# One product moved between two units of a Strassen stage, and new orders for its units

## The chip, the cores and the metric

The kernel runs on one core of a Trainium2 chip, as one launch. The metric is the device time of that launch in microseconds (us); the median of three runs is given. Matrix work is done by TensorE (PE), everything else by VectorE (DVE), ScalarE (ACT) and GpSimd (POOL); SyncE (SP) issues most of the transfers.

## The reference

A short causal convolution over time feeds a two-layer network with a hard-swish between. All arrays are float32.

```python
# x: (8, 4096, 192), weight: (8 heads, 7 taps)
w = softmax(weight, axis=-1)                  # exp(w - max), / (sum + 1e-9)
out[b, s, h, g] = sum_k w[h, k] * x_pad[b, s + k, h, g]   # 6 zeros ahead in time
x = out.reshape(32768, 192)

h = x @ w_in                                  # w_in (192, 2048)
g = h * clip(h + 3, 0, 6) / 6
return g @ w_out                              # w_out (2048, 192)
```

## The kernel before, in words

**Blocks.** The 32768 tokens are cut into 32 blocks of 1024. Block 0 is computed plainly, while the weights are still being prepared; blocks 1 to 31 all go through the same two stages, one after the other: the *h stage* (`h_phase`, lines 404 to 418), which makes `g`, and the *output stage* (`out_strassen`, lines 586 to 624; `out_last` for the last block), which makes the result and, on VectorE, the convolution of the next block.

**Two streams.** The 192 channels lie as three thirds of 64 rows. Rows 0 to 63 of the arrays hold the lower 512 tokens of a block and the lower half of `w_in`'s 2048 columns; rows 64 to 127 hold the upper ones. A matmul of the h stage (`half_mm`, line 303) uses 64 rows, so two run side by side on TensorE: stream **L** on the lower 64 rows, stream **U** on the upper 64. Each stream needs both token halves; a copy of `y` with the halves swapped (`OTHER`) is made by two transfers per block.

**Units and operations.** A *unit* is 2 x 128 columns of `w_in` for each stream; there are four (`UNITS`), numbered 1 to 4 here (0 to 3 in the code). The class `Unit` (line 355) has one object for each unit and stream. In a unit, the first two thirds of the channels are multiplied by Strassen's scheme with seven products instead of eight (`P1` to `P7`), on sums prepared of `y` (`YS1` to `YS4`) and of the weights (`w_in_t`). The last third is added plainly by `K11`, `K12`, `K21`, `K22`. That makes 11 products in a stream and unit, 44 in a stream and stage, each [64 x 128] by [64 x 512], into one of the eight PSUM banks. The operations have short names, with the stream's letter before them:

- `P1`: starts the bank of result a. `F1` (ScalarE, line 385): copies P1 from bank to bank, as the start of result b. `P6` accumulates onto that copy, so it waits for `F1`.
- `P5`: a bank of its own. `CE` (ScalarE, line 388): copies P5 to memory (`p5`, three buffers) and gives its bank back.
- `AF` and `AD` (VectorE, line 392): add P5 to what stands in b's bank, and write the sum as the start of result f, or d. `P7` goes onto b between the two, so it waits for `AF`; `K22` goes onto d and waits for `AD`. `P4` and `K21` finish b.
- `Ra`, `Rf`, `Rb`, `Rd` (ScalarE, line 317): the clipped factor of a result. `Ga`, `Gf`, `Gb`, `Gd` (VectorE, line 321): the gate, which multiplies by it, writes `g`, and gives the bank back.

Banks are handed out in the order in which they were given back (`take`, `give`, lines 297 to 301): which operation gives a bank that another takes follows from the order of the plan.

**What sets the order.** The order is written out by hand. `PLAN` (line 349) is a list of steps such as `LP6`; `h_phase` goes through it once for each unit and calls `run`, so each engine's instructions stand in its queue in this order. A step with `'` belongs to the unit before, so the last products and gates of a unit lie in the next unit's pass; such steps do nothing in the first pass, and a fifth pass at the end runs them alone. `X` runs what is left of the block before: its last transpose and its stores.

For the first unit of a stage, then, TensorE's queue begins `LP1 UP1 LP5 UP5 LP6 UP6 LP2 UK11`, and ScalarE's `LF1 UF1 LCE UCE`. From the second unit on, `LP4'` and `UP4'` of the unit before lie between P1 and P6 as well.

**The output stage** uses all 128 rows and a quarter of the columns for each of four products side by side (`mm`, line 423, recorded at line 427). It has 168 matmuls, needs both streams' results, and follows the h stage in TensorE's queue.

Of the kernel before, what the change touches and what calls it, by code (L numbers as in the profile page):

```python
# [16 lines left out]
def kernel(  # L17
# [101 lines left out]
    UNITS = NP // 2  # L119
# [214 lines left out]
    def h_out(c, group, bs, between):  # L334
# [11 lines left out]

    PLAN = """
        LP1 LRd' UP1 LGd' LP4' UP4' URd' LF1 LP5 UGd' UF1 UP5 LP6 UP6 LP2 LCE UCE LRb'  # L350
        UK11 LAF UAF LK11 X URb' UP2 LP7 LGb' UP7 LK12 UP3 UGb' LAD LP3 LRa URa LRf UK12
        UAD UGa LGa LK22 UK22 URf LGf UGf LK21 UK21
    """.split()

    class Unit:

# [45 lines left out]
                give(b)  # L402

    def h_phase(left):
        last = None
        for u in range(UNITS + 1):
            now = [Unit(u, k) for k in range(2)] if u < UNITS else None
            for step in PLAN:
                if step == "X":
                    while left:  # L410
                        left.pop(0)()
                    continue
                which = last if step[-1] == "'" else now
                if which:
                    which["LU".index(step[0])].run(step[1:].rstrip("'"))
            if last:
                g_sums(nc.gpsimd, (1, 3), range(2 * u - 2, 2 * u), 2)
            last = now

    def dff_half(k):  # L420
        return g[:, :, k // G, k % G]
# [55 lines left out]
    def g_sums(engine, which, slots, width):  # L477

        forms = {
            1: (S1, A21, A22, ALU.add), 3: (S3, A11, A21, ALU.subtract),  # L480
            2: (S2, S1, A11, ALU.subtract), 4: (S4, A12, S2, ALU.subtract),
        }
        for n in which:
            o, a, b, op = forms[n]
            for p in slots[::width]:
                r = slice(p, p + width)
                engine.tensor_tensor(out=o[:, r], in0=a[:, r], in1=b[:, r], op=op)  # L487
# [155 lines left out]
    with tc.manual_schedule():  # L643
# [106 lines left out]
        for i in range(1, NB):  # L750
            h_phase(left)
            if i + 1 < NB:
                left = out_strassen(i, conv_units(i + 1, [slice(0, K3)]))
            else:
                out_last(i)
            if i + 2 < NB:
                x_tiles[i + 2] = load_x(i + 2)
# [33 lines left out]
```

## Time and profile before

| | |
|---|---|
| time, median of 3 runs | 2425.71 us (2425.64 to 2425.78) |
| span of the profiled execution | 2423.9 us |
| TensorE's granted clock | 1.00 |
| h stage of a block, line 311 | 38.57 us |
| output stage of a block, line 427 | 36.19 us |
| VectorE busy in one h stage | 31.41 us |
| ScalarE busy in one h stage | 27.82 us |
| VectorE busy in one output stage | 33.72 us |

A page of the profile names groups of instructions by the line that issues them: L311 are all the h stage's matmuls, L427 those of the output stage, L385 the copies F1, L388 the copies CE, L392 AF and AD, L317 the clipped factors, L321 the gates. PE are the matmuls and PEld the weight loads that precede them. Each float32 matmul is recorded as two passes with a weight load each, and a few per cent of the records are missing. [...]the distance between starts says how fast they follow each other. "PE busy" is the time in which at least one matmul runs: two streams side by side and one stream alone look the same there.

### The profile page before, as it was taken

What the parts mean: (1) busy time and instruction counts of PE and PEld (TensorE: products, weight loads), DVE (VectorE), ACT (ScalarE), POOL (GpSimd) and SP (SyncE); (2) the same over time, 40 slices, a digit from 0 to 9 for tenths busy, and PEclk for the clock granted to TensorE, in tenths of its full rate; (3) what the DMA queues carried; (4) which work ended last, traced back from release to release, by engine and by line L of the source; (5) the groups of instructions that cost most, each with busy time, mean ns of one, the idle gap of its engine ahead of it and who ended that gap; (6) DMA issues with size and microseconds to landing.
All of it is one profiled execution on the core that took longest, in us unless ns stands there. A gap on an engine that the chain in (4) does not pass through costs nothing.

```text
span 2423.9 us, 40261 instructions
## 1 busy us (share of the span) xinstructions
PE 2413.0 (100%) x16468; PEld 1042.4 (43%) x16468; DVE 2088.9 (86%) x2534; ACT 1066.5 (44%) x1827; POOL 669.4 (28%) x280
## 2 busy tenths in 40 slices
PE   9999999999999999999999999999999999999998
PEld 4334444444444444443444444444444444344443
DVE  8788888988888888898888898888898888888886
ACT  7234553345443355433454334543345443355433
POOL 2423321233221333122332223322233312333122
PEclk9999999999999999999999999999999999999999
DMA  5211122201122111221112211122201122111210
GB/s 144 40 28 26 27 40 40 40 18 28 35 40 40 21 33 27 40 40 22 32 27 40 40 34 21 25 40 40 40 17 35 29 40 40 21 33 27 40 27 14
DMA packets 227338, 84.67 MB, mean 35 GB/s; under 512 B 205456, under 2 KB 210576, under 8 KB 227152
## 3 DMA queue, kind: packets, MB, share of 16 engines
q1 hardware_dynamic: 225848, 81.56, 17.1%
q8 instruction: 129, 2.11, 0.4%
q14 instruction: 57, 0.47, 0.1%
q10 hardware_dynamic: 1208, 0.27, 0.1%
q0 software_dynamic: 96, 0.26, 0.0%
HBM read 31.72 MB, written 25.17 MB: 23 GB/s over the span
## 4 chain that ended last, share of the span: by engine, by line
PE 99%; DVE 1%; DMA 0%; issue 0%; ACTq 0%; SPq 0%; DVEq 0%
PE psum L311 51%; PE psum L427 48%; DVE y L263 0%; DMA x<-in_x_dram 0%; DMA y<-y 0%; DVE c L531 0%; ACTq L92 0%; DVE scale L174 0%; DVE y L259 0%; DVE scale L195 0%; DVE sig L199 0%; DVE top L178 0%; DVE xt L537 0%; SPq L276 0%; DVEq L259 0%
## 5 line engine op out<-in xcount | busy, mean ns | idle before, releaser
L427 PE MATMUL psum<-g,w_out 128*32 128x512 f32 x9312 | 1163.6, 592 | 0.0
L311 PE MATMUL psum<-y,w_in 64*128 64x512 f32 x3664 | 957.2, 591 | 3.1 <-DVE y L263 1.7
L487 POOL TENSOR_TENSOR s<-g 128x1024 f32<-128x1024 f32 x124 | 293.4, 2366 | 1659.4 <-DVE g L321 1615.9
L317 ACT ACTIVATE r<-psum,half 128x512 f32<-128x512 f32 x1024 | 634.6, 688 | 241.6 <-PE psum L311 238.8
L427 PEld LDWEIGHTS psum<-g,w_out 128*32 128x32 f32 x9312 | 337.4, 110 | 811.7 <-issue 762.7
L321 DVE SCALAR_TENSOR_TENSOR g<-r,psum 128x512 f32<-128x512 f32 x1024 | 643.1, 681 | 4.4 <-ACT r L317 1.1
L427 PE MATMUL psum<-s,w_out 128*32 128x512 f32 x1488 | 638.5, 592 | 0.0
L311 PEld LDWEIGHTS psum<-y,w_in 64*128 64x128 f32 x3664 | 476.8, 187 | 345.0 <-issue 327.9
L311 PE MATMUL psum<-y,w_in_t 64*128 64x512 f32 x1984 | 610.2, 592 | 0.0
L392 DVE TENSOR_TENSOR psum<-psum,p 128x512 f32<-128x512 f32 x496 | 321.5, 694 | 198.7 <-PE psum L311 194.0
L263 DVE SCALAR_TENSOR_TENSOR y<-x,c_sb,y 128x1536 f32<-128x1536 f32 (+1 forms) x210 | 416.8, 1992 | 6.6
L523 ACT COPY c<-psum 32x512 f32<-32x512 f32 x188 | 108.9, 579 | 600.5 <-PE psum L427 511.7
L311 PEld LDWEIGHTS psum<-y,w_in_t 64*128 64x128 f32 x1984 | 280.1, 187 | 209.2 <-issue 142.4
L487 POOL TENSOR_TENSOR g<-g 128x1024 f32<-128x1024 f32 x124 | 336.2, 2711 | 9.7
L531 DVE TENSOR_TENSOR c<-c,psum 32x512 f32<-32x512 f32 (+1 forms) x187 | 128.1, 685 | 95.7 <-ACT c L523 89.8
L427 PEld LDWEIGHTS psum<-s,w_out 128*32 128x32 f32 x1488 | 162.4, 110 | 1.2 <-issue 1.2
L388 ACT COPY p<-psum 128x512 f32<-128x512 f32 x248 | 135.0, 587 | 61.8 <-PE psum L311 61.1
L385 ACT COPY psum<-psum 128x512 f32<-128x512 f32 x248 | 131.4, 571 | 62.3 <-PE psum L311 56.7
L487 DVE TENSOR_TENSOR g<-s,g 128x2048 f32<-128x2048 f32 x62 | 141.2, 2319 | 2.1 <-PE psum L427 2.1
L487 DVE TENSOR_TENSOR g<-g 128x2048 f32<-128x2048 f32 x62 | 139.4, 2289 | 2.3 <-PE psum L427 1.3
L591 ACT COPY c<-psum 96x512 f32<-96x512 f32 x30 | 17.5, 582 | 188.5 <-PE psum L427 188.5
L596 ACT COPY c<-psum 96x512 f32<-96x512 f32 x30 | 17.5, 583 | 170.0 <-PE psum L427 170.0
(46 smaller groups left out, 432.4 us busy)
## 6 DMA issues: line engine op xcount, KB each, us to landing
out_dram<-xt SPq DMA_DIRECT2D x382, 64.0 KB, 2.0
y<-y SPq DMA_DIRECT2D x62, 384.0 KB, 4.9
x<-in_x_dram SPq DMA_DIRECT2D x55, 388.5 KB, 5.9
stage<-in_moe_w_in_dram SPq DMA_DIRECT2D x16, 192.0 KB, 4.5
stage<-in_moe_w_out_dram SPq DMA_DIRECT2D x8, 384.0 KB, 5.6
x<-in_x_dram SPq DMA_DIRECT2D x7, 384.0 KB
y<-y SPq DMA_DIRECT2D x6, 128.0 KB, 2.4
x<-in_x_dram SPq DMA_DIRECT2D x2, 128.0 KB, 4.4
```

Of the source, the lines that this page charges most:

```text
L263: nc.vector.scalar_tensor_tensor(out=to, in0=x[:, part, k + t : k + t + W], scalar=c, in1=to, op0=ALU.mult, op1=ALU.add,)
L311: nc.tensor.matmul(out=psum[:, b], lhsT=w[r], rhs=y[r, third_of_y], start=start, stop=stop, skip_group_check=onto,)
L317: nc.scalar.activation(r6, h, ACT.Relu, bias=half[:], scale=1.0 / 6.0)
L321: nc.vector.scalar_tensor_tensor(out=out, in0=r6, scalar=1.0, in1=h, op0=ALU.min, op1=ALU.mult)
L385: nc.scalar.copy(out=psum[:, bank["b"]], in_=psum[:, bank["a"]])
L388: nc.scalar.copy(out=self.p5[:], in_=psum[:, bank["e"]])
L392: nc.vector.tensor_tensor(out=psum[:, to], in0=psum[:, bank["b"]], in1=self.p5[:], op=ALU.add)
L427: lambda p=p: nc.tensor.matmul(out=bank[j * QS : (j + 1) * QS], lhsT=w_out[:, p, w, cols], rhs=x[:, p], start=(first and p == ps_[0]), sto ...
L487: engine.tensor_tensor(out=o[:, r], in0=a[:, r], in1=b[:, r], op=op)
L523: nc.scalar.copy(out=dst[rows(q)], in_=src[rows(j)])
L531: nc.vector.tensor_tensor(out=out, in0=x, in1=y, op=op)
L591: nc.scalar.copy(out=p1[:], in_=bank[m])
```

## The change

The single `PLAN` becomes three: `FIRST` for the first unit, `SECOND` for the second, and `OTHERS` for the third, the fourth and the pass at the end. A new mark, `+`, says that a step belongs to the next unit; all `Unit` objects of a stage are therefore made at its beginning.

In the first unit there is no unit before, so no `P4'` lies between P1 and P6. `UP5+` is put there: the second unit's P5 of stream U is computed in the first unit, after `UP5` and ahead of `LP6` in TensorE's queue, and its copy `UCE+` comes after `UCE` and `LP2`. In the second unit, U then has no P5. The products themselves and their number stay the same. The rest of the change is the order of the steps, which is new in all three plans: in `OTHERS`, for example, U's P1 comes ahead of L's, and U's clipped factor of a ahead of L's.

```diff
-    PLAN = """
-        LP1 LRd' UP1 LGd' LP4' UP4' URd' LF1 LP5 UGd' UF1 UP5 LP6 UP6 LP2 LCE UCE LRb'
-        UK11 LAF UAF LK11 X URb' UP2 LP7 LGb' UP7 LK12 UP3 UGb' LAD LP3 LRa URa LRf UK12
-        UAD UGa LGa LK22 UK22 URf LGf UGf LK21 UK21
-    """.split()
+    FIRST = """
+        LP1 UP1 LP5 UP5 LF1 UF1 UP5+ LP6 LCE UCE UP6 LP2 UCE+ UK11 LAF LK11 UAF X UP2 LP7
+        LRa UP7 LK12 URa LAD UP3 LP3 UAD LGa UK12 LK22 LRf UGa UK22 LK21 URf LGf LRd UK21
+    """.split()
+    SECOND = """
+        LP1 UGf' URd' LGd' UP1 LP4' LF1 UGd' UP4' LP5 UF1 LP6 UP6 LCE LRb' LP2 UK11 LAF
+        URb' UAF LK11 UP2 LGb' LP7 UP7 URa UGb' LRa UP3 LK12 LAD UAD UK12 LP3 UGa LK22 UK22
+        LRf LGa URf LK21 UK21 LGf LRd
+    """.split()
+    OTHERS = """
+        UP1 UGf' LP1 URd' LGd' LP4' UP4' UGd' LF1 LP5 UP5 UF1 LP6 UP6 LCE UCE LP2 UK11 LAF
+        LRb' UAF LK11 UP2 URb' LGb' LP7 UP7 URa UGb' LRa LK12 UP3 LAD LP3 UAD UK12 UGa LK22
+        UK22 LRf LGa URf LK21 UK21 LGf LRd
+    """.split()
+    PLANS = [FIRST, SECOND] + [OTHERS] * (UNITS - 1)
...
     def h_phase(left):
-        last = None
-        for u in range(UNITS + 1):
-            now = [Unit(u, k) for k in range(2)] if u < UNITS else None
-            for step in PLAN:
+        work = {(u, k): Unit(u, k) for u in range(UNITS) for k in range(2)}
+        for u, plan in enumerate(PLANS):
+            for step in plan:
                 if step == "X":
                     while left:
                         left.pop(0)()
                     continue
-                which = last if step[-1] == "'" else now
-                if which:
-                    which["LU".index(step[0])].run(step[1:].rstrip("'"))
-            if last:
+                op = step[1:].rstrip("'+")
+                at = u + (step[-1] == "+") - (step[-1] == "'")
+                if at < UNITS:
+                    work[at, "LU".index(step[0])].run(op)
+            if u:
                 g_sums(nc.gpsimd, (1, 3), range(2 * u - 2, 2 * u), 2)
-            last = now
```

## The prediction

> **What bounds the kernel now.** I read the page's shares first, then the chain that ended last, then one output block in order of time. The page:
>
> ```profile
> PE 2413.0 (100%) x16468; PEld 1042.4 (43%) x16468; DVE 2088.9 (86%) x2534; ACT 1066.5 (44%) x1827; POOL 669.4 (28%) x280
> ...
> PE 99%; DVE 1%; DMA 0%; issue 0%; ACTq 0%; SPq 0%; DVEq 0%
> ```
>
> TensorE makes the time, but "100% busy" doesn't say that both halves of its array work: the h stage runs two streams side by side, L on rows 0 to 63 and U on rows 64 to 127, and one busy stream fills the row. The chain in order of time shows the stages:
>
> ```profile
> 1035.78 36.19 PE psum L427 x336
> 1071.97 38.57 PE psum L311 x175
> 1110.54 36.19 PE psum L427 x336
> ```
>
> The h stage (L311) takes 38.57 us and the output stage (L427) 36.19 us; every pair from the second on in this view has these two lengths, so what one h stage saves counts 31 times. Each stream has 44 products of two passes (each matmul is recorded twice). A pass that waits for nothing starts 0.429 us after the last (1074.70, 1075.13, 1075.56 below), so 88 passes need 88 x 0.429 = 37.8 us, about 0.8 us less than the stage takes. Where is that? The weight loads at a stage's start (columns: start, length, what, and in brackets the idle time before it and its releaser):
>
> ```profile
> 1071.90 0.30 PEld L311 LDWEIGHTS psum<-y,w_in 64*128 64x128 f32 x4 [0.84 <-issue]
> 1072.43 0.19 PEld L311 LDWEIGHTS psum<-y,w_in_t 64*128 64x128 f32 x2 [0.24 <-issue]
> 1072.86 0.19 PEld L311 LDWEIGHTS psum<-y,w_in_t 64*128 64x128 f32 x2 [0.24 <-issue]
> 1073.73 0.29 PEld L311 LDWEIGHTS psum<-y,w_in_t 64*128 64x128 f32 x2 [0.68 <-ACT psum L385]
> 1074.22 0.18 PEld L311 LDWEIGHTS psum<-y,w_in_t 64*128 64x128 f32 x1 [0.20 <-ACT psum L385]
> ...
> 1074.70 0.25 PEld L311 LDWEIGHTS psum<-y,w_in 64*128 64x128 f32 x2 [0.18 <-issue]
> 1075.13 0.25 PEld L311 LDWEIGHTS psum<-y,w_in 64*128 64x128 f32 x2 [0.18 <-issue]
> 1075.56 0.19 PEld L311 LDWEIGHTS psum<-y,w_in 64*128 64x128 f32 x1 [0.18 <-issue]
> ```
>
> Up to 1073 both streams go together (x2). Then L's P6 waits for its copy LF1 (released 1073.73) and U's P6 for UF1, which stands behind LF1 on ScalarE (1074.22):
>
> ```profile
> 1073.11 1.06 ACT L385 COPY psum<-psum 128x512 f32<-128x512 f32 x2 [0.50 <-PE psum L311]
> 1074.20 1.07 ACT L388 COPY p<-psum 128x512 f32<-128x512 f32 x2
> ```
>
> P5's second passes began at 1073.29 and 1073.30, so each half was free at about 1073.72. L lost 0.015 us of waiting plus 0.105 (a weight load that couldn't go ahead makes the first pass 0.534 long instead of 0.429: P6's passes start at 1073.735 and 1074.269), together 0.12. U lost 0.50 + 0.105 = 0.60. From there on U runs 0.49 behind, and no later wait of the stage takes that back or adds to it:
>
> ```profile
> 1109.03 0.59 PE L311 MATMUL psum<-y,w_in_t 64*128 64x512 f32 x1
> 1109.09 0.59 PE L311 MATMUL psum<-y,w_in 64*128 64x512 f32 x1
> 1109.46 1.08 PE L311 MATMUL psum<-y,w_in_t 64*128 64x512 f32 x3
> 1110.47 1.06 PE L427 MATMUL psum<-g,w_out 128*32 128x512 f32 x8
> ```
>
> L's last pass starts at 1109.46, U's at 1109.46 + 1.08 - 0.59 = 1109.95. The output stage needs both halves of the rows, so it starts behind U, 0.52 later at 1110.47; L stands still for 0.49 us. Check: L has 87 x 0.429 + 0.105 (the stage's first load) + 0.12 = 37.56, and 1109.46 - 1071.90 = 37.56; U has 38.05 in both ways.
>
> **What the Trainium skill says.** "TensorE: Matmul & The Clock Gate", Part 3 (packing small matmuls), says that a weight load overlaps a running matmul only when the row groups differ, and that matmuls start and end in program order. The trace agrees on the streams (pass starts 0.007 us apart while aligned, 0.06 while U lags). Whether a lone U product lets L's next one start half-way through isn't shown before, and this change rests on it. "TensorEngine Tiling (Array Packing)", Key Properties, says a change of tiling mode drains TensorE: the trace has 0.52 instead of 0.43 at both borders of the stage, which the change keeps. "PSUM — Partial Sum Buffer", section Engine vs sequencer instructions, calls the ScalarE and VectorE queues strict FIFO: UF1 behind LF1 agrees. "Perfetto Trace Analysis", Identifying Dependency Chains, says that waits on several engines add an event instruction ahead; the trace has such, 0.017 us with one condition and 0.038 with two.
>
> **The change part by part.** Nothing is added to the work: 88 passes a stream, 48 ScalarE and 48 VectorE operations a stage as before.
>
> *P5 of unit 2 into the gap.* U is free at 1073.726; the moved product takes two passes to 1074.584. UF1 is done by then (release 1074.22, 0.36 early), so UP6's load goes ahead and neither the 0.50 nor the 0.105 is paid. The 0.60 of loss in U goes in unit 1. Its bank is the seventh of eight taken in the stage, last read by the sum u3 at about 1142.6 to 1143.3 in a stage that ends at 1146.7: no wait. L's LP6 stands behind it in the program, but it dispatches at about 1073.30 (the start of UP5's second pass) and LP6 isn't released before 1073.73: no cost if the streams are as independent as above.
>
> *Where U stands then.* After UP6, U has done one product more and is 0.25 later than before; from unit 2 on, where L has P5 and U not, it is 0.60 earlier than before, hence level with L.
>
> *The extra ScalarE copy.* UCE+ comes at about 1075.17, behind UCE (start 1074.68), and ends by 1075.76; the queue's next, LRa, isn't released until 1076.61 and ScalarE idles 1.34 us there: hidden. p5 has three buffers, and three are live: no wait in the first unit. In the second, LCE reuses the first, read by LAF at 1075.3, six us before.
>
> *LF1's bank* is now one last read by an earlier VectorE sum. That wait is long over, but LF1's event now has two conditions: 0.038 - 0.017 = 0.02 more, on L's path (LP6). From 0 to 0.04; I take 0.02.
>
> *U's new gap in unit 2.* Its UP6 has only UP4 between itself and UP1. UP1's second pass starts at 1081.88 (1072.01, which is U's first pass with its exposed load, + 23 x 0.429); the quickest copy behind a pass here starts 0.62 after it (LF1 of unit 2, 1081.76 behind a pass at 1081.14), takes 0.57 and releases TensorE 0.05 later: 1083.12. U's turn is 1083.17. The load is 0.05 early; an exposed one costs 0.105, so about 0.05. ScalarE is free for it: LF1 runs 1081.76 to 1082.33, and UF1 isn't ready until 1082.50. Then UP7 waits for UAF, which follows LAF on VectorE: released at 1085.76 as in the rhythm of before (1085.01 + 0.69 + 0.05), U's turn 1085.80, up to 0.06. U's loss is then 0.05 + 0.06 = 0.11 against L's 0.12 + 0.02: L sets the end, U ties. In units 3 and 4 UAF comes about 0.10 ahead of UP7's turn: nothing, to 0.02.
>
> *The new order elsewhere* (loops U-first in units 3 and 4, bank waits LGa/UGa exchanged, UF1 behind UGd instead of LGd). UGd of unit 2 ended at 1091.89 before; UF1 from there ends at 1092.5, UP6's turn is 1092.7: hidden, by 0.14 at least. L's waits (LAF to LP7: 0.38 early; LAD to LK22: 0.8 early) keep their operations in the same order on VectorE.
>
> *After the stage.* The output stage starts earlier by what U no longer lags; its VectorE work doesn't (that follows L's last gates). The nearest product to wait there is the sixth or third, behind row sums that end 3.5 us or more ahead, and VectorE idles 2.64 us before its last sums. 0.47 is taken out of that slack.
>
> Sum per stage: 0.49 - 0.02 = 0.47. Times 31: 14.6 us. 2425.7 - 14.6 = 2411.1.
>
> **The rivals.** *A, the forecast:* L sets the end; saving 0.43 to 0.50, 2410 to 2412.5. For: both lanes' sums above close to 0.01 us. Chance 0.66.
> *B, U remains the later stream.* Its waits in units 2 to 4 are so near that small errors expose loads: 0.105 twice in unit 2 and 0.05 in units 3 and 4 each make U's loss 0.31 against 0.12, so 0.19 of the 0.49 stays: 31 x 0.30 = 9.3, 2416.4. For: leads of 0.05. Against: once U is late, its next waits are easier. Chance 0.18.
> *C, the streams are not that independent:* L's P6 must wait for the lone product's second pass (1074.16 instead of 1073.74), 0.42 late; 31 x 0.07 = 2, about 2423.5, within 0.2%. For: matmuls in program order. Against: the half-offset pairs through the whole stage before. Chance 0.08.
> *D, slower:* a bank or a gate in the new order holds L 0.4 in each of two units: 0.8 - 0.49 = 0.3 lost per stage, 2435. For: VectorE has 31.4 us of work in 38.6 here. Against: the slacks above. Chance 0.08.
>
> **How the numbers follow.** A gives 2411.1. Low: 0.50 + 0.02 a stage is the most that L's own sum allows, 2409.5. High: A and B with B's poorer half, 0.18 a stage, 2420. That leaves out C and D, 0.16. Faster is A and B, 0.84; same C; slower D.
>
> **What would show it.** Right: h stages of about 38.1 and output stages of 36.19 in the chain; no load idle of 0.68 for both streams at once, UP6 loading without exposure; at the stage's end both streams' last passes within 0.1 us. Wrong: LP6 later than 1.84 us after the stage's first load (C); U last by 0.2 or more, with loads released by L385 or L392 in unit 2 (B); output stages over 36.3 (VectorE late); L waits for gates (D).

## The result, and the profile after

The changed kernel takes 2410.9 us (2410.75 to 2410.95, six runs) against 2425.7 us (2425.64 to 2425.78, six runs of the kernel before beside it): 14.8 us less, a ratio of 0.9939 with a 95% interval of 0.9926 to 0.9952. The forecast was 2411.1.

The page's first line after, which again can't show the gain as a share:

```profile
PE 2399.2 (100%) x16468; PEld 1008.8 (42%) x16468; DVE 2088.8 (87%) x2534; ACT 1077.1 (45%) x1827; POOL 671.3 (28%) x280
```

The chain that ended last, in order of time (start, length, work), for the same block as before. L437 is the output stage; the change moved the line numbers:

```profile
1029.51 36.19 PE psum L437 x336
1065.69 38.08 PE psum L311 x174
1103.77 36.19 PE psum L437 x336
```

The h stage is 0.49 us shorter, 38.08 instead of 38.57; the output stage is what it was. The stage's first weight loads (start, length, what, and the idle time before them with its releaser):

```profile
1065.62 0.30 PEld L311 LDWEIGHTS psum<-y,w_in 64*128 64x128 f32 x4 [0.84 <-issue]
1066.16 0.19 PEld L311 LDWEIGHTS psum<-y,w_in_t 64*128 64x128 f32 x2 [0.24 <-issue]
1066.59 0.19 PEld L311 LDWEIGHTS psum<-y,w_in_t 64*128 64x128 f32 x2 [0.23 <-issue]
1067.02 0.19 PEld L311 LDWEIGHTS psum<-y,w_in_t 64*128 64x128 f32 x1 [0.24 <-issue]
1067.45 0.29 PEld L311 LDWEIGHTS psum<-y,w_in_t 64*128 64x128 f32 x3 [0.24 <-ACT psum L396]
1067.94 0.18 PEld L311 LDWEIGHTS psum<-y,w_in_t 64*128 64x128 f32 x1 [0.20 <-ACT psum L396]
```

The load at 1067.02, a single one, is new: it is UP5+, 1.40 us after the stage's first load, and there is no 0.68 us of idle any more. At 1067.45 stand three loads: LP6's, released by LF1 as before, UP5+'s second, and LP6's second. UP6's load at 1067.94 is still released by UF1, but U's half is busy until 1068.31, so nobody waits. The end of the stage:

```profile
1102.32 0.60 PE L311 MATMUL psum<-y,w_in 64*128 64x512 f32 x2
1102.75 1.02 PE L311 MATMUL psum<-y,w_in_t 64*128 64x512 f32 x4
1103.70 1.06 PE L437 MATMUL psum<-g,w_out 128*32 128x512 f32 x8
```

The streams' last four passes go in two pairs, 0.43 apart (a pass is recorded with 0.59, so the last starts at 1102.75 + 1.02 - 0.59 = 1103.18), and the output stage follows 0.52 later. Before, U's last pass stood alone.

None of the 176 passes of an h stage is missing from these traces. They can be told apart by the order of the queue, by the weight tile's name and by the distance of at least 0.429 us within a stream (where both streams wait for the same kind of tile within 0.1 us, which of them it was follows from the waits). A pass's *turn* is the moment 0.429 us after the pass before it in its stream. The table has what each stream lost against its turns, in us; the reasons and the experiments rest on it. Every stage also has 0.10 for its first load, left out here:

| kernel | L | U | h stage | time |
|---|---|---|---|---|
| before | P6 of unit 1: 0.12 | P6 of unit 1: 0.60 | 38.57 | 2425.7 |
| after | P6 of unit 1: 0.11; P7 of unit 3: 0.01 | P6, P7 of unit 2: 0.07, 0.03; P7 of unit 3: 0.01 | 38.08 | 2410.9 |
| only the move | P6 of unit 1: 0.12 | P6, P7 of unit 2: 0.07, 0.04; P5 of unit 3: 0.19 | 38.27 | 2416.7 |
| only the orders | P6 of unit 1: 0.11 | P6 of unit 1: 0.59 | 38.56 | 2425.6 |
| move, and UP5 ahead of UF1 | P6 of unit 1: 0.12; P7 of unit 3: 0.01 | P6, P7 of unit 2: 0.07, 0.04; P7 of unit 3: 0.01 | 38.09 | 2411.7 |
| L's product moved | P6 of unit 2: 0.06 | P6, P7 of unit 1: 0.60, 0.25 | 38.83 | 2433.7 |
| both moved | P6 of unit 2: 0.07 | P6 of unit 2: 0.55 | 38.52 | 2424.0 |

### The profile page after: what moved, and what is told of

Its sections match the earlier page's. It is cut to its first block, busy times and chain, and to the rows that moved or that the text cites. A ratio compares the mean times of both kernels' runs of the same rounds, so it can differ in the third digit from the quotient of the medians.

```text
span 2409.1 us, 40076 instructions
## 1 busy us (share of the span) xinstructions
PE 2399.2 (100%) x16468; PEld 1008.8 (42%) x16468; DVE 2088.8 (87%) x2534; ACT 1077.1 (45%) x1827; POOL 671.3 (28%) x280
## 4 chain that ended last, share of the span: by engine, by line
PE 99%; DVE 1%; DMA 0%; issue 0%; ACTq 0%; SPq 0%; DVEq 0%
PE psum L311 50%; PE psum L437 48%; DVE y L263 0%; DMA x<-in_x_dram 0%; DMA y<-y 0%; DVE c L541 0%; ACTq L92 0%; DVE scale L174 0%; DVE y L259 0%; DVE sig L199 0%; DVE scale L195 0%; DVE top L178 0%; DVE xt L547 0%; SPq L276 0%; DVEq L259 0%
## 5 line engine op out<-in xcount | busy, mean ns | idle before, releaser
L437 PE MATMUL psum<-g,w_out 128*32 128x512 f32 x9312 | 1163.6, 592 | 0.0
L311 PE MATMUL psum<-y,w_in 64*128 64x512 f32 x3664 | 885.1, 592 | 2.1 <-DVE y L263 1.9
L317 ACT ACTIVATE r<-psum,half 128x512 f32<-128x512 f32 x1024 | 641.3, 688 | 241.3 <-PE psum L311 234.2
L437 PEld LDWEIGHTS psum<-g,w_out 128*32 128x32 f32 x9312 | 337.4, 110 | 811.7 <-issue 769.9
L437 PE MATMUL psum<-s,w_out 128*32 128x512 f32 x1488 | 638.5, 592 | 0.0
L311 PEld LDWEIGHTS psum<-y,w_in 64*128 64x128 f32 x3664 | 430.2, 187 | 378.7 <-issue 299.4
L311 PE MATMUL psum<-y,w_in_t 64*128 64x512 f32 x1984 | 523.8, 592 | 0.0
L311 PEld LDWEIGHTS psum<-y,w_in_t 64*128 64x128 f32 x1984 | 247.1, 186 | 194.3 <-issue 124.9
L396 ACT COPY psum<-psum 128x512 f32<-128x512 f32 x248 | 138.9, 571 | 72.6 <-PE psum L311 57.4
L437 PEld LDWEIGHTS psum<-s,w_out 128*32 128x32 f32 x1488 | 162.4, 110 | 1.2 <-issue 1.2
```

The lines of the kernel that those rows point to most:

```text
L311: nc.tensor.matmul(out=psum[:, b], lhsT=w[r], rhs=y[r, third_of_y], start=start, stop=stop, skip_group_check=onto,)
L317: nc.scalar.activation(r6, h, ACT.Relu, bias=half[:], scale=1.0 / 6.0)
L396: nc.scalar.copy(out=psum[:, bank["b"]], in_=psum[:, bank["a"]])
L437: lambda p=p: nc.tensor.matmul(out=bank[j * QS : (j + 1) * QS], lhsT=w_out[:, p, w, cols], rhs=x[:, p], start=(first and p == ps_[0]), sto ...
```

## The experiments

In all of them the same work is done; only the order of its steps differs and, where it is said, the number of p5 buffers.

### The parts of the change

**Only the move.** Before's order everywhere, with the product and its copy moved:

```diff
-        LP1 UP1 LF1 LP5 UF1 UP5 LP6 UP6 LP2 LCE UCE UK11 LAF UAF
+        LP1 UP1 LF1 LP5 UF1 UP5 UP5+ LP6 UP6 LP2 LCE UCE UCE+ UK11 LAF UAF
...
-        LP1 LRd' UP1 LGd' LP4' UP4' URd' LF1 LP5 UGd' UF1 UP5 LP6 UP6 LP2 LCE UCE LRb'
+        LP1 LRd' UP1 LGd' LP4' UP4' URd' LF1 LP5 UGd' UF1 LP6 UP6 LP2 LCE LRb'
```

> Before's order of steps in every unit; only UP5 of the second unit is moved into the first unit's gap, with its copy. Theory (the filled gap is the whole gain): h stage about 38.1 us, time 2411 us, within 1.5 of the changed kernel. Rival (the newly searched orders are needed, since U, no longer late, runs into its waits for UF1, UAF and the exchanged banks): U ends 0.2 or more behind L, h stage 38.3 or more, 2417 us or more.

Measured: 2416.7 us (2416.57 to 2416.8; before 2425.66), ratio 0.9963 (0.995 to 0.9976). The theory fails and the rival comes close: its 2417 and its 38.3 were 0.3 us and 0.03 us too high, and of the waits that it named only that for a bank makes the difference. The move alone is worth 8.9 of the 14.8 us. U loses nothing in unit 1. The chain's piece for this block (the stage is 0.19 longer than after):

```profile
1067.94 38.27 PE psum L311 x176
```

But U runs level with L now, and its P5 of unit 3 takes the bank that UGd of unit 2 gives back. VectorE in this kernel, the last two gates of that unit (LGd and UGd):

```profile
1086.58 1.28 DVE L321 SCALAR_TENSOR_TENSOR g<-r,psum 128x512 f32<-128x512 f32 x2
```

They end at 1087.86, and UP5's first pass starts at 1087.92, 0.08 behind its turn and with an exposed load, one that can't go ahead of its pass (0.10 more). In the kernel before, the same gate ended at the same place of the stage, but U came 0.49 later: its lag had hidden the wait.

**Only the orders.** The changed kernel's three plans with UP5 back in the second unit:

```diff
-        LP1 UP1 LP5 UP5 LF1 UF1 UP5+ LP6 LCE UCE UP6 LP2 UCE+ UK11 LAF LK11 UAF X UP2 LP7
+        LP1 UP1 LP5 UP5 LF1 UF1 LP6 LCE UCE UP6 LP2 UK11 LAF LK11 UAF X UP2 LP7
...
-        LP1 UGf' URd' LGd' UP1 LP4' LF1 UGd' UP4' LP5 UF1 LP6 UP6 LCE LRb' LP2 UK11 LAF
+        LP1 UGf' URd' LGd' UP1 LP4' LF1 UGd' UP4' LP5 UP5 UF1 LP6 UP6 LCE UCE LRb' LP2 UK11 LAF
```

> The changed kernel's three orders, but UP5 of the second unit is back in the second unit. Theory: U again waits 0.50 us for UF1 and loads exposed (0.105), ends 0.49 behind L; h stage 38.57, time 2425.5 us, within 1 of the kernel before. Rival (the orders carry part of the gain): below 2422 us.

Measured: 2425.6 us (2425.49 to 2425.67; before 2425.66), ratio 1.0 (0.9991 to 1.0008). The orders bring nothing alone: U waits its 0.49 in unit 1 again, and the chain has the old stage:

```profile
1071.82 38.56 PE psum L311 x175
```

So the parts don't add: 0 and 8.9 make 14.8.

**The move, and one exchange.** Which part of the new orders is it? To the kernel with only the move, one step was exchanged in units 3 and 4, so that UP5 takes the bank of LGd and UF1 that of UGd:

```diff
-        LP1 LRd' UP1 LGd' LP4' UP4' URd' LF1 LP5 UGd' UF1 UP5 LP6 UP6
+        LP1 LRd' UP1 LGd' LP4' UP4' URd' LF1 LP5 UGd' UP5 UF1 LP6 UP6
```

> The kernel with only the product moved (2416.7 us, U's P5 of unit 3 waited for a bank that UGd gives back, 0.08 + 0.10 us), with one more exchange in units 3 and 4: UP5 ahead of UF1 in the plan, so that UP5 takes the bank that LGd gives, 0.6 us earlier, and UF1 the one of UGd. Theory (that handover is all that the searched orders were needed for): h stage 38.08 to 38.10, time 2411 us, within 1. Rival (the gates' and clipped factors' order, U first, is needed too): 2414 us or more.

Measured: 2411.7 us (2411.64 to 2411.8; before 2425.76), ratio 0.9942 (0.9927 to 0.9957). The exchange alone brings 5.0 of the missing 5.8 us, and UP5's wait is gone from the table:

```profile
1066.08 38.09 PE psum L311 x175
```

Of the 0.8 that is left, its usual stage of 38.09 explains 0.3, and rare longer stages (below) 0.5 in the profiled execution. The rest of the new orders has no size that these runs can show.

### Which stream, and which queue

**L's product moved instead of U's**, in before's order:

```diff
-        LP1 UP1 LF1 LP5 UF1 UP5 LP6 UP6 LP2 LCE UCE UK11 LAF UAF
+        LP1 UP1 LF1 LP5 UF1 UP5 LP5+ LP6 UP6 LP2 LCE UCE LCE+ UK11 LAF UAF
...
-        LP1 LRd' UP1 LGd' LP4' UP4' URd' LF1 LP5 UGd' UF1 UP5 LP6 UP6 LP2 LCE UCE LRb'
+        LP1 LRd' UP1 LGd' LP4' UP4' URd' LF1 UGd' UF1 UP5 LP6 UP6 LP2 UCE LRb'
```

> Before's order; the product moved is L's P5 of the second unit instead of U's. Theory: the later stream sets the end, and U keeps its loss of 0.60 us a stage: h stage 38.57, time 2425.7 us, within 1. Rival (a filled TensorE gap pays in whichever stream it lies, since less of TensorE idles): L's loss of 0.12 us a stage is won, 31 x 0.12 = 3.7, time 2422 us.

Measured: 2433.7 us (2433.47 to 2433.73; before 2425.66), ratio 1.0033 (1.002 to 1.0046): slower, which neither expected. L's loss in unit 1 goes and brings nothing, as the theory had it, for U keeps its 0.60. But U loses 0.25 more at P7. LP6 comes 0.84 later (2.68 instead of 1.84 after the stage's beginning), so LAF starts later, and UAF stands behind it on VectorE. This kernel's stage began at 1075.20:

```profile
1079.01 1.30 DVE L398 TENSOR_TENSOR psum<-psum,p 128x512 f32<-128x512 f32 x2 [0.34 <-PE psum L311]
```

LAF starts 3.81 after the stage's beginning, 3.39 before; UAF follows at 4.41 instead of 3.99 and is done at 5.10, when UP7's turn was 5.01.

**UAF first.** Only this pair is exchanged against that kernel (`LAF UAF` to `UAF LAF` in the first unit).

> L's product moved, before's order (2433.7 us, 8 slower than before), with UAF ahead of LAF in the first unit. Theory (LP6 comes 0.85 later there, so LAF 0.41 later, and UAF and UP7 stood behind it on VectorE, 0.25 us a stage): that 0.25 goes, U keeps its 0.60, time 2425.7 us, within 1. Rival (the moved product itself holds U up, by the order on TensorE): stays at 2433 us.

Measured: 2435.1 us (2435.03 to 2435.21; before 2425.76), ratio 1.0039 (1.0024 to 1.0054). The theory, as far as it named VectorE alone, fell: U's loss at P7 rose to 0.30. The rival, with the order on TensorE, comes nearer, 2 us short. The stage began at 1075.98, and UAF started 3.85 after that:

```profile
1079.83 0.70 DVE L398 TENSOR_TENSOR psum<-psum,p 128x512 f32<-128x512 f32 x1 [0.38 <-PE psum L311]
```

Yet UP6's second pass had begun at 2.86. LP6, which stands ahead of UP6 in TensorE's queue, began its second pass at 3.11, 0.74 ahead of UAF. That fits a wait for a count of finished products in the order of the queue, which is reached only when LP6 is done too. And UP7 was late although UAF was done at 4.55: it stood behind LP7, whose load waited for LAF (done at 5.14) and came at 5.20; UP7's load followed 0.01 later.

**U ahead in both queues.** So UP6, UP7 and UK22 were put ahead of L's on TensorE, and UAF and UAD on VectorE:

```diff
-        ... LP5+ LP6 UP6 ... UAF LAF LK11 X UP2 LP7 UP7 LK12 UP3 LAD LP3 ... UK12 UAD UGa LGa LK22 UK22
+        ... LP5+ UP6 LP6 ... UAF LAF LK11 X UP2 UP7 LP7 LK12 UP3 UAD LP3 ... UK12 LAD UGa LGa UK22 LK22
```

> L's product moved as in the run with UAF first (2435.1 us), and now U stands ahead of L in the first unit on both engines: UP6, UP7 and UK22 ahead of L's on TensorE, UAF and UAD on VectorE. Theory (a waiting step of the later stream L holds up whatever stands behind it in the same queue, and VectorE's count of finished products makes UAF wait for LP6 as long as LP6 stands ahead of UP6): U's extra 0.30 us a stage goes, its 0.60 for UF1 stays, h stage 38.57, time 2425.7 us, within 1. Rival (a product moved in L costs U by sharing the array): above 2430 us.

Measured: 2425.8 us (2425.66 to 2425.82; before 2425.66), ratio 1.0 (0.9992 to 1.0009). The 0.30 is gone and the 0.60 is there: U's losses are again those of before, L has 0.07, and the time is that of before. UAF starts 3.56 after the stage's beginning (1071.99), only 0.45 after LP6's second pass:

```profile
1075.55 0.70 DVE L398 TENSOR_TENSOR psum<-psum,p 128x512 f32<-128x512 f32 x1
```

So UAF doesn't need LP6 where LP6 stands behind UP6. A product moved in the stream that isn't the later one is worth nothing, and what it cost came through the order in the queues. These exchanges were made together, so their single shares stay open.

### Is there more to win?

**Both moved**, with four p5 buffers. L's P5 goes ahead of UP5+ in the changed kernel's first plan, and its copy ahead of UCE+:

```diff
-        LP1 UP1 LP5 UP5 LF1 UF1 UP5+ LP6 LCE UCE UP6 LP2 UCE+ UK11
+        LP1 UP1 LP5 UP5 LF1 UF1 LP5+ UP5+ LP6 LCE UCE UP6 LP2 LCE+ UCE+ UK11
...
-        LP1 UGf' URd' LGd' UP1 LP4' LF1 UGd' UP4' LP5 UF1 LP6 UP6 LCE LRb'
+        LP1 UGf' URd' LGd' UP1 LP4' LF1 UGd' UP4' UF1 LP6 UP6 LRb'
```

> The changed kernel with L's P5 of the second unit moved as well (four p5 buffers). In unit 1 L then loses nothing. In unit 2 only P4 lies between P1 and P6 in both streams, which are level now, and UF1 stands 0.49 us behind LF1 on ScalarE. Theory: U's loss of about 0.5 to 0.6 us comes back in unit 2: h stage 38.5, time about 2424 us. Rival (the gap of unit 1 is what costs, and with both filled L's 0.12 goes too): 31 x 0.1 = 3 less than the changed kernel, 2408 us.

Measured: 2424.0 us (2423.92 to 2424.15; before 2425.66), ratio 0.9993 (0.9984 to 1.0002). The wait moves from unit 1 to unit 2. Its weight loads there:

```profile
1082.51 0.29 PEld L311 LDWEIGHTS psum<-y,w_in_t 64*128 64x128 f32 x2 [0.62 <-ACT psum L393]
1083.00 0.18 PEld L311 LDWEIGHTS psum<-y,w_in_t 64*128 64x128 f32 x1 [0.20 <-ACT psum L393]
```

It is the picture of before's unit 1: LP6 at the first copy's end, UP6 0.49 later at the second's. Two copies in one queue serve two level streams 0.49 apart; one product between P1 and P6 as a filler covers the first, two cover both (the next run). The changed kernel escapes since U is 0.75 behind L when unit 2 begins, so that its copy starts (10.61 after the stage's beginning) when LF1 has ended (10.42).

**Both moved, and a second filler in unit 2** (K21 of unit 1 moved behind P4'):

```diff
-        LP1 UGf' URd' LGd' UP1 LP4' LF1 UGd' UP4' UF1 LP6 UP6
+        LP1 UGf' URd' LGd' UP1 LP4' LF1 UGd' UP4' LK21' UK21' UF1 LP6 UP6
```

> Both streams' P5 of unit 2 moved into unit 1 (four p5 buffers, 2424.0 us with that alone), and K21 of unit 1 in both streams moved behind P4 in unit 2, so that two products lie between P1 and P6 there. Theory (what is left of a stage's loss is only waits for F1 without a filler): L's 0.12 us a stage goes, U's in unit 2 as well, up to 0.06 for UP7 stays: 31 x 0.06 to 0.12, time 2407.2 to 2409 us. Rival (something else now sets the end, gates or banks): 2410.9 us or more.

Measured: 2417.2 us (2417.04 to 2417.32; before 2425.76), ratio 0.9965 (0.9952 to 0.9977). L loses nothing now, and no P6 waits. But the unit is two passes shorter, and UP1 of unit 2 comes before UGa has given its bank: the gate ends 8.86 after the stage's beginning, UP1 starts at 8.92, 0.22 late and 0.10 for its load. The stage is the rival's:

```profile
1068.44 38.29 PE psum L311 x176
```

**U first in unit 2**, so that UP1 takes LGa's bank and L does P4 before P1:

```diff
-        LP1 UGf' URd' LGd' UP1 LP4' LF1 UGd' UP4' LK21' UK21' UF1 LP6 UP6 ... LAF URb' UAF ... LP7 UP7
+        UP1 UGf' URd' LGd' LP4' UP4' LP1 UGd' UK21' UF1 LK21' LF1 UP6 LP6 ... UAF URb' LAF ... UP7 LP7
```

> Both products and K21 of unit 1 moved (2417.2 us, where UP1 of unit 2 waited 0.22 + 0.10 us for the bank of UGa), with U ahead in unit 2: UP1 takes LGa's bank at once, L does P4 first and then P1, which takes UGa's bank 0.86 later; UF1 stands ahead of LF1, UP6, UAF and UP7 ahead of L's. Theory: U loses nothing, L only has K21 between P1 and P6 and loses about 0.06: stage 38.03, 31 x 0.05 = 1.6 less than the changed kernel, 2409.3 us. Rival (another bank or gate takes the place of UGa's): 2411 us or more.

Measured: 2416.8 us (2416.7 to 2416.83; before 2425.66), ratio 0.9963 (0.995 to 0.9976). The bank's wait is gone, and another has its place: UF1 stood behind URd on ScalarE and started at 10.32, LF1 at 10.84, and P6 of one stream waited until 11.47, 0.20 late; a K22 then waited 0.14 for its AD. Each of the two had a load exposed besides (0.10).

**URd and UGd behind both copies**, and UAD and UK22 ahead of L's:

```diff
-        UP1 UGf' URd' LGd' LP4' UP4' LP1 UGd' UK21' UF1 LK21' LF1 UP6 LP6 ... LAD UAD ... LK22 UK22
+        UP1 UGf' LGd' LP4' UP4' LP1 UK21' UF1 LK21' LF1 URd' UGd' UP6 LP6 ... UAD LAD ... UK22 LK22
```

> As the run with U first (2416.8 us), where UF1 of unit 2 stood behind URd on ScalarE and LP6 waited 0.20 + 0.10 us for LF1, and LK22 waited 0.14 + 0.10 for an AD at the end of its line. Now URd and UGd come behind both copies, and UAD and UK22 ahead of LAD and LK22. Theory (these two waits are all that stood between it and its sum): only L's 0.06 for P6 of unit 2 is left beside the stage's first load; stage 38.03, 2409.3 us. Rival (URd, 1.3 us later, hands a wait on to the next in its queue, UAF or LRb): 2411 us or more.

Measured: 2410.6 us (2410.51 to 2410.75; before 2425.7), ratio 0.9938 (0.9924 to 0.9952), between the two expectations. Both waits are gone; P6 of unit 2 and P7 of unit 3 each start with a load exposed by 0.10, one in each stream, and the stage is where the changed kernel's is:

```profile
1065.60 38.09 PE psum L311 x175
```

That is 0.3 us less than the changed kernel, each beside its own runs of before, which agree within 0.1 us: no difference that counts. 0.12 us a stage is all that the changed kernel's later stream still loses beside its first load, and each of these four orders found a new wait for the one it removed.

## Why the prediction was right

**The bound and the gap.** As forecast: what counted was U's lag at the stage's end, 0.49 us, not the 0.12 and 0.60 lost in the streams. The run with L's product moved and U ahead shows it from the other side. The two check sums of the streams in the prediction come to 37.55 and 38.03 with the terms printed there, 0.01 and 0.02 short of what it reads, so they close a little less well than it says.

**UP5 in the gap.** As forecast to 0.01 us: UP5+'s passes start 1.827 and 2.257 after the stage's first matmul and UP6's at 2.686 (forecast 1.827, and 2.685 for UP6). LP6 wasn't held up (1.827): the one thing that no trace had shown, a lone product in one stream with the other's next starting half-way, holds. The p5 buffer that LCE takes in unit 2 is read last by LAD, not by LAF as the prediction has it; LAD had ended 5.4 us earlier in the changed kernel, so the conclusion stands.

**The order of matmuls.** The prediction took from the Trainium skill, "TensorE: Matmul & The Clock Gate", Part 3, that matmuls start and end in program order, and that a weight load overlaps a running matmul only when the row groups differ. Here the measurements differ from both. With L's product moved and UAF first, UP6 starts at 2.33 and LP6, ahead of it in the queue, at 2.68; UP6's second pass is first too (2.86 and 3.11). In order are their loads, 2.25 for LP6 and 2.33 for UP6. And UP5+'s second load begins with UP5+'s own first pass, both at 1067.45 in the changed kernel, so it overlaps a matmul of its own rows.

**The two-condition wait of LF1**, costed at 0.02 us, cost nothing: LF1 starts 1.204 after the stage's beginning, 1.214 before. That term was mis-sized; without it a usual stage saves 0.49 and not 0.47. The prediction had read it from the recorded lengths of the events ahead of the copies, 0.017 and 0.038; LF1's event now has two conditions and is recorded with 1.02 us, most of it waiting, so its length is no price.

**U's new gap in unit 2.** P6 lost 0.066 (forecast 0.05), P7 0.032 (forecast 0.06), 0.10 in all against 0.11. L and U end together, L last by 0.006. That was the step on which rival B hung, and it was as near as said: the kernel with only the move is rival B, 2416.7 us where B's sum was 2416.4, though not through the waits that B named.

**The new order elsewhere** was costed at nothing, with the bank waits among what the slacks hide. For the changed kernel that is right. What the prediction missed is why: it took the exchange of bank waits for a risk and gave before's order no part in it. With before's order, UP5 of unit 3 would have lost 0.19 to UGd; handing it LGd's bank is worth 5.0 us.

**The output stage** stayed at 36.19 in all of these runs, and VectorE has 2.16 us of idle time left before its last sums, instead of 2.64, as forecast.

**The sum.** 31 x 0.47 = 14.6 was forecast and 14.8 measured. By its terms that is 14.26 from 29 stages with 0.49 each, 0.42 from the first stage (it had lost less before: 38.52), and 0.14 from one stage (38.43, last section). So the agreement to 0.2 us is in part luck: without the 0.02 for the event the forecast would have been 15.2, and the first stage and that one stage took back 0.4 that it didn't have.

## What to carry to other kernels

Where two streams share an engine and are joined at a stage's end, price an edit by the stream that arrives last: filling the other's gap won nothing here, and cost 8 us through the queues. A stream that stops being late meets every wait that its lag had covered, so look up who hands it its buffers and which step stands ahead in each queue before you count the gain; here one exchange of two steps was a third of it. Each waiting step needs enough other work ahead of it for its producer's whole queue, the second copy included, and moving a filler moves the wait to where it was taken from.

## What was not expected of the hardware

VectorE now and then starts an operation 0.35 us late, with nothing in the trace that it waits for. One such place is the AF of unit 4 in block 26, in the profiled executions of both kernels and of several of the others; with only the move, and with the exchange, that stage is 38.44. VectorE's adds before, in block 25 and in block 26 (in brackets the idle time ahead of them):

```profile
1925.63 1.30 DVE L392 TENSOR_TENSOR psum<-psum,p 128x512 f32<-128x512 f32 x2 [1.96 <-PE psum L311]
```

```profile
2000.74 1.30 DVE L392 TENSOR_TENSOR psum<-psum,p 128x512 f32<-128x512 f32 x2 [2.31 <-ACT p L388]
```

And after, in block 26, with the chain's pieces from the same stretch:

```profile
1988.56 1.30 DVE L403 TENSOR_TENSOR psum<-psum,p 128x512 f32<-128x512 f32 x2 [2.31 <-ACT p L399]
```

```profile
1956.89 38.43 PE psum L311 x174
1995.32 36.19 PE psum L437 x336
2031.51 38.08 PE psum L311 x174
```

The idle time grows from 1.96 to 2.31 in both. The releaser named, a copy of ScalarE, ended 0.2 us before the late add; in block 25 the same add started 0.15 ahead of the end of that copy, so it doesn't need it. LAF and UAF both come late by it. L's P7 has its load in time in both kernels. Before, U ran 0.49 behind, and its P7 lost nothing either; after, U's P7 starts 0.25 behind its turn with an exposed load (0.10), and this one stage is 38.43 instead of 38.08. A tighter stage pays for stalls that a looser one hides. What the stall is, these runs don't show; ScalarE has similar ones of 0.28 us.
